# A decayed recurrence in halves of 64 steps, as 64x64 products, in a fused recurrence and expert kernel

## The chip, the cores and the metric

The kernel runs on one core of a Trainium2 chip. The metric is the time of one execution on the device, in microseconds (us). Engines are named as in the profile: PE is TensorE's matrix multiplication, PEld its weight load, DVE is VectorE, ACT is ScalarE, POOL is GpSimd, and SP is SyncE, which here only issues DMAs. [...]

## The reference

Two blocks follow each other. The first is a recurrence with a decaying state for each of 4 batches and 8 heads, with 768 steps and heads of 48; the second sends each of the 3072 resulting rows to one of 16 experts.

```python
B, H, S, D = 4, 8, 768, 48
for t in range(S):
    kt, vt, rt = k[:, :, t], v[:, :, t], r[:, :, t]
    cur = einsum('bhd,bhe->bhde', u[None] * kt, vt)
    y[:, :, t] = einsum('bhd,bhde->bhe', rt, state + cur)
    state = w[None, :, :, None] * state + einsum('bhd,bhe->bhde', kt, vt)

x = y.transpose(0, 2, 1, 3).reshape(B * S, H * D)      # 3072 x 384
# group g of 4 and expert e of 4 by the largest logit; gate = softmax(group) * softmax(expert)
out[token] = gate * (relu(x[token] @ w1[g, e]) @ w2[g, e])   # F = 1024
```

All is fp32.

## The kernel before

**The recurrence.** A tile is 128 steps of one batch with all 8 heads, so there are 6 chunks c times 4 batches b, 24 tiles, in the order of chunks. Two tiles (two batches of one chunk) make a pair g, loaded by three DMAs on SP: r, k and v, two pairs ahead. `SPAN` is 3: powers of the decay are folded into r and k (tables `T1T` and `T2`), so that the state needs a decay only after every third chunk. Heads lie in slots of 64 (`DP`), so that two heads e = 0, 1 fill 128 partitions; `HP` = 4 such double heads hc make up the 8 heads.

One loop over steps s writes the order on every engine by hand (`manual_schedule`): each engine takes its instructions exactly in the order of the program. Step s works on several tiles at different stages:

- `turn(s)` (L569): four transposes of r into bank `pr` and four of scaled k into `pk`. DVE multiplies `pr` by the decay powers into `rT`; ACT copies `pk` to `kT`.
- `own_values` (L560): eight small ACT instructions make `dv`, the part of a step's own k and v. `own_sum` (L556) is the DVE sum it starts from; POOL makes its products `dg` in `own` (L550).
- `rows_T(s-4)` and `row_logits(s-5)`: three transposes of finished rows into `px`, an ACT copy to `xT`, and six short product instructions for the router's logits.
- `back(s-3)` (L637): four transposes of `yT` into `pb`; DVE adds `dv` and writes the rows `xt`.
- `values(s-2)` (L596): the result `py` of a tile. First the state's part, `R` times `rT`, in full 128x128 products (a double head's two 48x48 states on the diagonal of `R`, zeros elsewhere, L605); then the part inside the tile, `vt` times the masked products `am` (L611). ACT copies `py` to `yT` (L616). Then the state's update `pu`, `kh` times `vt` (L622), which DVE adds to `R` (L630 to L635).
- `scores(s-1)` (L582): products of `kT` and `rT` (128 by 128 steps for each head) into two banks `pa`, which DVE multiplies by the mask `later` into `am` (L594).

Every fourth tile a routing follows, spread over the next steps by the dictionary `todo`: `choice` on DVE with one exp on ACT (at s = 9, 13, 17, 21, between `own_values` and `rows_T`), then in the next step `before` (two products into a bank `pre`, ahead of `turn`), `gate` and `place` at the step's end (`place` is the last to read `pre`), and then scatters of rows to DRAM by POOL. Towards the end the routings of the last chunk come two tiles at a time.

**PSUM.** Six banks turn round for everything (`bank`); two more (`route_bank`) hold logits. A new tile takes a bank as soon as all that used it are done:

```python
psum = ctx.enter_context(tc.tile_pool(name="psum", bufs=6, space=bass.MemoryType.PSUM))
rpsum = ctx.enter_context(tc.tile_pool(name="rpsum", bufs=2, space=bass.MemoryType.PSUM))
```

**The experts.** Seventeen items (the first expert in two parts) follow, each as: `columns` (transposes into `px`), `up` (four times, banks `ph`, L506), `down` (three times, bank `po`, L520) and `rows_out` (transposes into `pb`, then a scatter of rows by POOL). The first item is worked on inside the last steps of the recurrence. Weights of the next expert are loaded meanwhile.

Of the kernel before, what the change touches and what calls it, by code (L numbers as in the profile page):

```python
# [8 lines left out]
FP32 = mybir.dt.float32  # L9
# [25 lines left out]
def kernel(  # L35
# [46 lines left out]
    psum = ctx.enter_context(tc.tile_pool(name="psum", bufs=6, space=bass.MemoryType.PSUM))  # L82

    rpsum = ctx.enter_context(tc.tile_pool(name="rpsum", bufs=2, space=bass.MemoryType.PSUM))

    def bank(shape, name):
        return psum.tile(shape, FP32, tag="bank", name=name)
# [72 lines left out]

    first_use = cst([P, 1], "first_use")
# [16 lines left out]
    R = ring([P, HP, P], "R", B)  # L178
# [22 lines left out]
    for t in R:  # L201
        nc.gpsimd.memset(t, 0.0)
# [126 lines left out]
    def route_bank():  # L329

        return rpsum.tile([P, 512], FP32, tag="route", name="rb")
# [144 lines left out]
    def columns(i):  # L476
        xg, w = xgs.pop(i), width(i)
        xe = xes[i] = item_tile(i, [P, KO, room(i)], "xe")
        for ks in (range(0, KO),) if KO * w <= 512 else (range(0, 2), range(2, KO)):
            px = bank([P, len(ks), w], "px")  # L480
            for q, ko in enumerate(ks):
                for j, n in enumerate(parts(i)):
                    nc.tensor.transpose(  # L483
                        px[:, q, P * j : P * j + n], xg[0:n, j, P * ko : P * (ko + 1)], ident[0:n, 0:n]
                    )
            nc.vector.tensor_copy(xe[:, ks[0] : ks[-1] + 1, 0:w], px)  # L486
        ids = item_tile(i, [P, 2], "ids", U32, bufs=4)
        gates = item_tile(i, [P, 2], "gates", bufs=4)
        for j, n in enumerate(parts(i)):
            nc.vector.tensor_scalar(  # L490
                out=ids[0:n, j : j + 1], in0=xg[0:n, j, DM + ROW_ID : DM + ROW_ID + 1], scalar1=float(N),
                scalar2=None, op0=OP.add,
            )
            nc.vector.tensor_copy(gates[0:n, j : j + 1], xg[0:n, j, DM + ROW_GATE : DM + ROW_GATE + 1])
        keys_of[i] = ids, gates

    def up(i, f):
# [5 lines left out]
        ph = bank([P, 2, w], "ph")  # L503
# [8 lines left out]
    def down(i, d):  # L512
# [5 lines left out]
        po = bank([P, w], "po")  # L518
# [6 lines left out]
    def rows_out(i):  # L525
        y, (ids, gates) = yo.pop(i), keys_of.pop(i)
        for j, n in enumerate(parts(i)):
            pb = bank([P, DM], "pb")
# [52 lines left out]

    def scores(n):  # L582
        kT, rT = rkT[n]
        am = ams[n] = pool.tile([P, 2, HP, P], FP32, tag="am", bufs=2, name="am")
        pa = [bank([P, HP, P], f"pa{e}") for e in range(2)]
        for hc in range(HP):
            for e in range(2):
                rows = slice(DP * e, DP * e + D)
                nc.tensor.matmul(  # L589
                    pa[e][:, hc, :], lhsT=kT[rows, hc, :], rhs=rT[rows, hc, :],  # L590
                    start=True, stop=True, skip_group_check=True,
                )
        for e in range(2):
            nc.vector.tensor_mul(am[:, e], pa[e], spread(later, 1, HP))  # L594

    def values(n):  # L596
# [3 lines left out]
        vt, kh = vts[g % (RING + 1)], khs[g % (RING - 1)]  # L600
        rT, am = rkT.pop(n)[1], ams.pop(n)
        py = bank([P, HP, P], "py")
        if c > 0:
            for hc in range(HP):
                nc.tensor.matmul(  # L605
                    py[:, hc, :], lhsT=R[b][:, hc, :], rhs=rT[:, hc, :], start=(hc == 0), stop=False,
                    skip_group_check=True,
                )
        for hc in range(HP):
            for e in range(2):  # L610
                nc.tensor.matmul(  # L611
                    py[DP * e : DP * (e + 1), hc, :], lhsT=vt[:, a, 2 * hc + e, :], rhs=am[:, e, hc, :],
                    start=(c == 0), stop=True, skip_group_check=True,
                )
        yT = yTs[n] = pool.tile([P, HP, P], FP32, tag="yT", bufs=2, name="yT")
        nc.scalar.copy(yT, py)  # L616
        if c == NCH - 1:
            return
        pu = bank([P, HP, D], "pu")
        for hc in range(HP):  # L620
            for e in range(2):
                nc.tensor.matmul(  # L622
                    pu[DP * e : DP * (e + 1), hc, :], lhsT=kh[:, a, 2 * hc + e, :], rhs=vt[:, a, 2 * hc + e, 0:D],
                    start=True, stop=True, skip_group_check=True,
                )
        for e in range(2):
            rows = slice(DP * e, DP * (e + 1))
            state = R[b][rows, :, DP * e : DP * e + D]
            if c == 0:
                nc.vector.tensor_copy(state, pu[rows])  # L630
            elif c % SPAN < SPAN - 1:
                nc.vector.tensor_add(state, pu[rows], state)
            else:
                nc.vector.tensor_add(pu[rows], pu[rows], state)
                nc.vector.tensor_mul(state, pu[rows], spread(w_span[rows, :], 2, D))  # L635
# [55 lines left out]
    for s in range(NT + LAST):  # L691
# [25 lines left out]
        if s < NT:  # L717
            turn(s)
            if s % 2 == 1 and s // 2 + 1 < NP:
# [3 lines left out]
        for n in range(NT):  # L723
            if s == max(n + 1, 2):
                own_values(n)
# [13 lines left out]
        if 0 <= s - 1 < NT:  # L739
            scores(s - 1)  # L740
# [310 lines left out]
```

## Time and profile before

| | us |
|---|---|
| median of 3 runs | 480.31 (479.12 to 485.27) |
| the profiled execution, its own time | 479.58 |
| its span from the first to the last instruction | 477.9 |
| PE busy | 449.7 |
| DVE busy | 159.5 |
| ACT busy | 139.0 |
| POOL busy | 129.5 |

Busy times are sums over an engine's instructions where overlapping ones count once; a matrix product's end is modelled, so PE's busy time also holds short gaps. Line numbers (L605) are those of the kernel before, and names such as `py<-am,vt` say what is written from what. For the pace of TensorE the starts of successive groups in the order of time are more reliable than the lengths of single instructions, which overlap.

### The profile page before, as it was taken

How to read it: one execution, taken by the hardware profiler on the slowest of the kernel's cores; microseconds unless marked ns; L12 is line 12 of the kernel's file. 1: busy time of each engine (PE TensorE's matmuls, PEld its weight loads, DVE VectorE, ACT ScalarE, POOL GpSimd, SP SyncE). 2: the span in 40 equal slices, each digit the busy share in tenths (PEclk: the TensorE clock that was granted, in tenths of full speed). 3: DMA queues.
4: the chain of work that ended last, by engine and by line, in shares of the span. 5: the costliest groups of instructions: out<-in, count | busy, mean ns of one | idle time of the engine just before them, and what ended most of it. 6: DMA issues, size and time to landing. Idle time of an engine off the chain costs nothing. (4 is left out here: it accounts for less than half of the span.)

```text
span 477.9 us, 9090 instructions
## 1 busy us (share of the span) xinstructions
PE 449.7 (94%) x3623; PEld 430.6 (90%) x3623; DVE 159.5 (33%) x478; ACT 139.0 (29%) x418; POOL 129.5 (27%) x135
## 2 busy tenths in 40 slices
PE   3799999999999898999999999999999999999992
PEld 2598888899999798999999999999999999999991
DVE  5546566877778663010110210110110110111000
ACT  2846553564656321111121111111111111111120
POOL 7834536556564042000010210110120110120011
PEclk9969979999999989999999999999999999999997
DMA  9999999983102994565465754755856765666000
GB/s 176 187 190 228 207 227 202 200 155 77 36 35 69 339 335 132 188 239 168 160 190 182 256 184 153 280 201 156 284 190 198 255 188 199 238 202 236 30 22 26
DMA packets 112024, 86.24 MB, mean 180 GB/s; under 512 B 79633, under 2 KB 103568, under 8 KB 111976
## 3 DMA queue, kind: packets, MB, share of 16 engines
q1 hardware_dynamic: 98920, 68.81, 52.1%
q10 hardware_dynamic: 8432, 7.31, 7.1%
q0 software_dynamic: 4624, 9.48, 5.8%
q8 instruction: 30, 0.49, 0.5%
q14 instruction: 18, 0.15, 0.1%
HBM read 69.79 MB, written 16.12 MB: 180 GB/s over the span
## 5 line engine op out<-in xcount | busy, mean ns | idle before, releaser
L534 POOL DMA_INDIRECT out_dram<-yt,ids x32 | 34.1, 1066 | 255.0 <-DVE yt L532 250.4
L506 PE MATMUL ph<-xe,w 128*128 128x128 f32 (+7 forms) x432 | 72.2, 325 | 0.7 <-DVE xe L486 0.7
L520 PE MATMUL po<-hT,w 128*128 128x128 f32 (+7 forms) x432 | 71.4, 322 | 0.0
L506 PEld LDWEIGHTS ph<-xe,w 128*128 128x128 f32 x432 | 69.0, 194 | 1.2 <-DVE xe L486 0.9
L532 DVE TENSOR_SCALAR yt<-pb,gates 128x384 f32<-128x384 f32 (+15 forms) x32 | 18.3, 611 | 153.4 <-PE pb L530 153.4
L520 PE MATMUL po<-hT,rall 128*128 128x240 f32 (+7 forms) x384 | 68.6, 336 | 0.0
L506 PE MATMUL ph<-xe,kall 128*128 128x240 f32 (+7 forms) x384 | 68.4, 335 | 0.0
L520 PEld LDWEIGHTS po<-hT,w 128*128 128x128 f32 x432 | 67.8, 190 | 0.5
L510 ACT ACTIVATE hT<-ph 128x256 f32<-128x256 f32 (+15 forms) x68 | 33.5, 493 | 112.9 <-PE ph L506 112.9
L520 PEld LDWEIGHTS po<-hT,rall 128*128 128x128 f32 x384 | 65.0, 190 | 0.7
L506 PEld LDWEIGHTS ph<-xe,kall 128*128 128x128 f32 x384 | 64.9, 190 | 0.6
L523 ACT COPY yo<-po 128x128 f32<-128x128 f32 (+15 forms) x51 | 16.3, 320 | 127.7 <-PE po L520 127.7
L564 ACT ACTIVATE dv<-vt,du 128x48 f32<-128x48 f32 x192 | 45.8, 324 | 1.1 <-DVE du L558 1.0
L594 DVE TENSOR_TENSOR am<-pa,later 128x512 f32<-128x512 f32 x48 | 30.9, 685 | 9.0 <-PE pa L589 8.7
L486 DVE COPY xe<-px 128x384 f32<-128x384 f32 (+30 forms) x32 | 14.0, 475 | 53.6 <-PE px L483 53.6
L410 POOL DMA_INDIRECT x_sorted<-xt,place_i x24 | 23.8, 990 | 27.9 <-issue 14.0
L589 PE MATMUL pa<-rT,kT 48*128 48x128 f32 x384 | 29.3, 291 | 0.7 <-DVE xt L646 0.7
L611 PE MATMUL py<-am,vt 128*64 128x128 f32 x384 | 29.2, 290 | 0.7 <-DVE am L594 0.6
L553 POOL TENSOR_TENSOR dg<-rall,kall 128x768 f32<-128x768 f32 x12 | 21.9, 1821 | 28.9 <-DVE du L558 28.9
L548 POOL TENSOR_TENSOR kh<-kall,T 128x768 f32<-128x768 f32 (+1 forms) x12 | 21.4, 1788 | 28.0 <-DMA kall<-in_k_dram 9.7
L611 PEld LDWEIGHTS py<-am,vt 128*64 128x64 f32 x384 | 22.7, 143 | 4.7 <-DVE am L594 1.5
L589 PEld LDWEIGHTS pa<-rT,kT 48*128 48x128 f32 x384 | 24.4, 193 | 2.6 <-DVE xt L646 0.9
(128 smaller groups left out, 469.6 us busy)
## 6 DMA issues: line engine op xcount, KB each, us to landing
w<-in_moe_w_dram SPq DMA_DIRECT2D x16, 1536.0 KB, 6.8
kall<-in_moe_w_dram SPq DMA_DIRECT2D x8, 1536.0 KB, 7.1
rall<-in_moe_w_dram SPq DMA_DIRECT2D x8, 1536.0 KB, 6.8
x_sorted<-nothing ACTq DMA_DIRECT2D x4, 1544.0 KB, 10.2
rall<-in_r_dram SPq DMA_DIRECT2D x12, 384.0 KB, 7.2
vt<-in_v_dram SPq DMA_DIRECT2D x12, 384.0 KB, 6.8
kall<-in_k_dram SPq DMA_DIRECT2D x10, 384.0 KB, 6.4
xg<-x_sorted SPq DMA_DIRECT2D x17, 193.0 KB, 6.2
```

What stands on the lines that cost most here:

```text
L410: ins = nc.gpsimd.indirect_dma_start(out=xs_dram, out_offset=bass.IndirectOffsetOnAxis(ap=place_i[:, i : i + 1], axis=0), in_=xt[:, i, :], ...
L506: nc.tensor.matmul(ph[:, q, :], lhsT=w1[:, ko, P * (f + q) : P * (f + q + 1)], rhs=xe[:, ko, 0:w], start=(ko == 0), stop=(ko == KO - 1), s ...
L510: nc.scalar.activation(hTs[i][:, f : f + 2, 0:w], ph, AF.Relu)
L520: nc.tensor.matmul(po, lhsT=w2[:, fo, P * d : P * (d + 1)], rhs=hT[:, fo, 0:w], start=(fo == 0), stop=(fo == FO - 1))
L532: nc.vector.tensor_scalar(out=yt[0:n], in0=pb[0:n], scalar1=gates[0:n, j : j + 1], scalar2=None, op0=OP.mult)
L534: ins = nc.gpsimd.indirect_dma_start(out=out, out_offset=bass.IndirectOffsetOnAxis(ap=ids[0:n, j : j + 1], axis=0), in_=yt[0:n], in_offset ...
L548: engine.tensor_mul(khs[g % (RING - 1)][:, a0:a1, :, 0:D], kts[g % RING][:, a0:a1], spread(T2[m], 1, a1 - a0))
L553: nc.gpsimd.tensor_mul(dg, rts[g % RING][:, :, :, 0:D], kts[g % RING])
L564: nc.scalar.mul(dv[:, h, :], vts[g % (RING + 1)][:, a, h, 0:D], dvs[g][:, a, h : h + 1])
L589: nc.tensor.matmul(pa[e][:, hc, :], lhsT=kT[rows, hc, :], rhs=rT[rows, hc, :], start=True, stop=True, skip_group_check=True,)
L594: nc.vector.tensor_mul(am[:, e], pa[e], spread(later, 1, HP))
L611: nc.tensor.matmul(py[DP * e : DP * (e + 1), hc, :], lhsT=vt[:, a, 2 * hc + e, :], rhs=am[:, e, hc, :], start=(c == 0), stop=True, skip_gr ...
```

## The change

A tile of 128 steps keeps its loads, its transposes and its tables. Inside it the recurrence goes in two halves q of 64 steps:

- Scores and values are formed only inside a half: 64x64 products (48 rows for the scores), and each product names one quarter of the array by the half of the partitions that it reads and the half that it writes. `am` has half the width, and the mask is a 64-wide one for both halves, `later_half`, filled by two ACT copies.
- The state is needed at the tile's start and in its middle. `R` becomes a ring of three states for each batch, without the empty diagonal blocks; `from_state` multiplies it by `rT` in 64x64 products, in the two diagonal quarters.
- The state's update leaves `values` and becomes `update(s)`, right after `turn(s)` in a tile's first step, with two products (one for each half) and two DVE additions (one in the last chunk, where the kernel before had none). It shares two banks with the scores of the same step.
- `from_state(s-1)` is called ahead of `scores(s-1)`, one step before `values` completes the same banks `py`, of which there are now two for a tile, one for each half. Each half is copied by ACT on its own.
- `own_values(n)` runs at s = n+2 and no longer at s = max(n+1, 2).
- PSUM is one pool of four names with two slots each: "bank" (pr, pk, px, pb, pre and others in the recurrence), "scores", "values" and "route". The expert stage is spread over the same names.

The diff, with the main parts:

```diff
-    psum = ctx.enter_context(tc.tile_pool(name="psum", bufs=6, space=bass.MemoryType.PSUM))
-    rpsum = ctx.enter_context(tc.tile_pool(name="rpsum", bufs=2, space=bass.MemoryType.PSUM))
-    def bank(shape, name):
-        return psum.tile(shape, FP32, tag="bank", name=name)
+    psum = ctx.enter_context(tc.tile_pool(name="psum", bufs=2, space=bass.MemoryType.PSUM))
+    def bank(shape, name, tag="bank"):
+        return psum.tile(shape, FP32, tag=tag, name=name)
...
+    HALF = P // 2
+    later_half = cst([P, HALF], "later_half")
+    for a in range(2):
+        rows = slice(HALF * a, HALF * (a + 1))
+        nc.scalar.copy(later_half[rows, :], later[rows, rows])
...
-    R = ring([P, HP, P], "R", B)
+    R = [ring([P, HP, DP], f"R_{b}", 3) for b in range(B)]
-    for t in R:
-        nc.gpsimd.memset(t, 0.0)
+    for t in sum(R, []):
+        nc.gpsimd.memset(t[:, :, D:DP], 0.0)
...
-            px = bank([P, len(ks), w], "px")
+            px = bank([P, len(ks), w], "px", "route" if i > 0 else "bank")
-        ph = bank([P, 2, w], "ph")
+        ph = bank([P, 2, w], "ph", "bank" if f % 4 == 0 else "scores")
-        po = bank([P, w], "po")
+        po = bank([P, w], "po", "values")
...
+    def update(n):
+        c, b = tiles[n]
+        g, a = n // 2, n % 2
+        vt, kh = vts[g % (RING + 1)], khs[g % (RING - 1)]
+        pu = [t[:, HP * HALF :].rearrange("p (c d) -> p c d", c=HP) for t in both]
+        halves = 2 if c < NCH - 1 else 1
+        for hc in range(HP):
+            for q in range(halves):
+                half = slice(HALF * q, HALF * (q + 1))
+                for e in range(2):
+                    nc.tensor.matmul(
+                        pu[q][DP * e : DP * (e + 1), hc, :], lhsT=kh[half, a, 2 * hc + e, :],
+                        rhs=vt[half, a, 2 * hc + e, 0:D], start=True, stop=True, skip_group_check=True,
+                    )
+        for q in range(halves):
+            old, new = state(n, q)[:, :, 0:D], state(n, q + 1)[:, :, 0:D]
+            if c == 0 and q == 0:
+                nc.vector.tensor_copy(new, pu[q])
+            elif q == 0 or c % SPAN < SPAN - 1:
+                nc.vector.tensor_add(new, pu[q], old)
+            else:
+                nc.vector.tensor_add(pu[q], pu[q], old)
+                nc.vector.tensor_mul(new, pu[q], spread(w_span, 2, D))
...
+    def from_state(n):
+        c, b = tiles[n]
+        rT = rkT[n][1]
+        py = pys[n] = [bank([P, HP, HALF], f"py{q}", "values") for q in range(2)]
+        for q in range(2):
+            if c == 0 and q == 0:
+                continue
+            half = slice(HALF * q, HALF * (q + 1))
+            for hc in range(HP):
+                for e in range(2):
+                    rows = slice(DP * e, DP * (e + 1))
+                    nc.tensor.matmul(
+                        py[q][rows, hc, :], lhsT=state(n, q)[rows, hc, :], rhs=rT[rows, hc, half],
+                        start=(hc == 0), stop=False, skip_group_check=True,
+                    )
...
     def scores(n):
-        am = ams[n] = pool.tile([P, 2, HP, P], FP32, tag="am", bufs=2, name="am")
-        pa = [bank([P, HP, P], f"pa{e}") for e in range(2)]
+        am = ams[n] = pool.tile([P, 2, HP, HALF], FP32, tag="am", bufs=2, name="am")
+        pa = [t[:, 0 : HP * HALF].rearrange("p (c t) -> p c t", c=HP) for t in both]
...
+                for q in range(2):
+                    half = slice(HALF * q, HALF * (q + 1))
+                    nc.tensor.matmul(
+                        pa[e][half, hc, :], lhsT=kT[rows, hc, half], rhs=rT[rows, hc, half],
+                        start=True, stop=True, skip_group_check=True,
+                    )
...
     def values(n):
+                    nc.tensor.matmul(
+                        py[q][DP * e : DP * (e + 1), hc, :], lhsT=vt[half, a, 2 * hc + e, :], rhs=am[half, e, hc, :],
+                        start=(c == 0 and q == 0), stop=True, skip_group_check=True,
+                    )
-        nc.scalar.copy(yT, py)
+        for q in range(2):
+            nc.scalar.copy(yT[:, :, HALF * q : HALF * (q + 1)], py[q])
...
         if s < NT:
             turn(s)
+        if s <= NT:
+            both = [bank([P, HP * (HALF + D)], f"pa{e}", "scores") for e in range(2)]
+        if s < NT:
+            update(s)
...
-            if s == max(n + 1, 2):
+            if s == n + 2:
                 own_values(n)
...
         if 0 <= s - 1 < NT:
+            from_state(s - 1)
             scores(s - 1)
```

## The prediction

> **What bounds the kernel now.** I read the page first (which engine, which stretch), then the sums over windows, then the order in time of one step of the recurrence, and last one step in which ScalarE and VectorE are late.
>
> ```profile
> span 477.9 us, 9090 instructions
> PE 449.7 (94%) x3623; PEld 430.6 (90%) x3623; DVE 159.5 (33%) x478; ACT 139.0 (29%) x418; POOL 129.5 (27%) x135
> ...
> PEclk9969979999999989999999999999999999999997
> ...
> L594 DVE TENSOR_TENSOR am<-pa,later 128x512 f32<-128x512 f32 x48 | 30.9, 685 | 9.0 <-PE pa L589 8.7
> ...
> L611 PE MATMUL py<-am,vt 128*64 128x128 f32 x384 | 29.2, 290 | 0.7 <-DVE am L594 0.6
> ```
> TensorE bounds the kernel in both stages: the experts from about 180 us on, which the change touches only in the names of PSUM slots, and before that 24 tiles of recurrence, one a step. Each fp32 product is two instructions (384 for 192), so I count instructions.
>
> ```profile
> 22.33:32.57 10.24, 9.63 (x72) 8.64 (x73) 5.40 (x10) 5.77 (x22) 4.60 (x5) 0.50 1.16 186
> ...
> 66.70:73.53 6.83, 6.83 (x34) 6.52 (x35) 1.88 (x4) 2.75 (x10) 0.29 (x1) 0.50 1.20 199
> 114.27:120.66 6.39, 6.33 (x83) 5.96 (x81) 6.00 (x20) 3.26 (x12) 5.04 (x4) 1.00 0.02 9
> ```
> These are sums by window: length, busy PE, PEld, DVE, ACT, POOL, then the granted clock. Twice the clock was halved, after TensorE had been idle (18.8 to 21.7; 0.73 us and more just before 65.06). The third line is an undisturbed step: PE full, DVE nearly so.
>
> A plain step in order of time (start, length, engine):
>
> ```profile
> 120.77 0.61 PE L575 MATMUL pr<-ident,rall 128*128 128x128 f32 x4
> ...
> 121.22 0.60 PE L575 MATMUL pk<-ident,kh 128*128 128x128 f32 x4
> ...
> 121.65 0.49 PE L438 MATMUL px<-ident,xt 128*128 128x128 f32 x3
> ...
> 121.98 0.74 PE L443 MATMUL rb<-gw,xT 128*128 128x20 f32 x6
> ...
> 122.57 0.64 PE L645 MATMUL pb<-ident,yT 128*128 128x128 f32 x4
> ...
> 123.04 1.06 PE L605 MATMUL py<-rT,R 128*128 128x128 f32 x8
> ...
> 124.03 1.09 PE L611 MATMUL py<-am,vt 128*64 128x128 f32 x16
> ...
> 124.95 0.62 PE L622 MATMUL pu<-vt,kh 128*64 128x48 f32 x16
> 125.22 0.59 ACT L616 COPY yT<-py 128x512 f32<-128x512 f32 x1 [0.56 <-PE py L611]
> 125.50 0.97 PEld L589 LDWEIGHTS pa<-rT,kT 48*128 48x128 f32 x16
> 125.50 1.16 PE L589 MATMUL pa<-rT,kT 48*128 48x128 f32 x16
> ...
> 126.60 0.44 PE L575 MATMUL pr<-ident,rall 128*128 128x128 f32 x2
> ```
> From start to start: turn 0.88 (0.93 after a step with pa), px 0.33, logits 0.59, pb 0.47, state product 0.99, py 0.92, pu 0.55, pa 1.10; 5.83 together, 5.87 in most steps. Nothing waits: yT is copied while TensorE already does pu and pa, because py may lie in one of six banks.
>
> A step with a routing choice, on DVE and ACT:
>
> ```profile
> 116.84 0.23 DVE L363 TENSOR_REDUCE mx<-rb 128x20 f32<-128x80 f32 x1
> ...
> 119.52 0.23 DVE L376 TENSOR_TENSOR ex<-rb,mx 128x80 f32<-128x80 f32 x1
> ...
> 119.79 0.27 ACT L377 ACTIVATE ex<-ex 128x80 f32<-128x80 f32 x1 [1.94 <-DVE ex L376]
> 119.97 0.46 ACT L439 COPY xT<-px 128x384 f32<-128x384 f32 x1
> 120.33 0.59 ACT L616 COPY yT<-py 128x512 f32<-128x512 f32 x1
> ```
> The choice holds DVE for 2.9 us, ACT waits in order for its exp, and yT comes 6.06 us after the step's start (114.27), when TensorE has finished the whole step. Here that costs almost nothing.
>
> [...] two-at-once groups take 57 ns an instruction (L611) against 124 for L605, single starts lie in pairs 6 ns apart, and mode changes cost 0.05 to 0.15 us. Four at once is not shown. [...] The halved stretches here are 10.24 and 6.83 us[...].
>
> **The change part by part.** *Products.* Instructions a tile: before 8+16+16+16, after 32 each for state, values, update, scores. In L622 a pair of 64-column loads repeats every 58 ns in the trace[...]. Four at once I take at the same 58 to 60 ns a round: 8 rounds are 0.48, 0.6 with a mode change, for update and values; 0.6 for scores with the change back. Bounds: 0.5, and 0.95 if only two ever run together. from_state uses only the two diagonal quarters: 16 rounds of 58, 0.95. Sum 2.75 against 3.56: TensorE saves 0.8 us a step, 0.3 in the first and last four tiles (the first now have half a state product, the last half an update). About 15 us in all if no wait came.
>
> *Wait A, the banks of py.* from_state(s-1) needs both "values" banks, which values(s-2), just ahead of it on TensorE, has filled. So TensorE waits for the result (0.29 after the last start, from L622's 0.27), the first half's copy (0.36, from 0.46 at 384 columns and 0.36 at 240), 0.06 for the signal and 0.05 for weights: about 0.65 a step more. Behind it stand from_state, scores and the next step. This takes most of the 0.8.
>
> *Wait B, update against the masks.* update(s) comes right after turn and needs the "scores" banks that the am products of the step before are reading. At half width these are 0.42 each (0.685 at 512, 0.553 at 384 columns); they end 1.0 after the step's start, turn 0.93. Cost 0.13. rT follows at 1.6, when update ends, so px, which takes pr's bank, does not wait. A plain step: 0.93+0.13+0.6+0.33+0.59+0.47+0.6+0.65+0.95+0.6 = 5.85. No gain.
>
> *Choice steps (s = 9, 13, 17, 21).* DVE has the adds of update first (to 2.5), then 2.9 us of choice: 5.4. exp, xT, then yT's first half end near 6.3; only then from_state (0.95) and scores (0.6): 7.95, 2.1 more than plain.
>
> *Steps with pre first (10, 14, 18, 22).* pre keeps one of the two "bank" slots until the place product at the step's end, so pr, pk, px, pb share one. pr ends at 0.94; pk waits for rT (1.99); update to 3.0; px waits for kT (3.36); pb waits for xT, which stands behind eight dv on ACT (5.5); values to 6.6, wait A, from_state to 8.2, scores 8.8. That is 2.5 over 6.3. The next step loses 0.3 because gate and place hold DVE ahead of am.
>
> Four steps thus take 5.87+7.95+8.8+6.15 = 28.8, four times 115.2 for s = 8 to 23. Before they took 103.6 (from step starts at 52.6 and 156.2), 4.6 of it through the halved clock: 11.6 more.
>
> *Clock.* Each choice step leaves TensorE idle for 2.7 us, like the gaps of 2.9 and 3.0 that were followed by halving, and the pre step after it idles again. Step 10 and 11 lost 4.6 us to 6.8 us of half clock; with waits as cover I take 3 us for each of four: 12. Bounds 0 and 20.
>
> *The rest.* Early on, update(3) waits for am(1), which stands behind the reduce of dg on DVE (until 22.2): one part step later, 1.5. own_values one step later frees yT(0) on ACT, but that only lets TensorE reach the same wait. v is needed two steps earlier; its loads land 4.3 to 13.2 us after issue and are issued four steps ahead, so no wait. The two later_half copies (0.2 each) fall into ACT's 4.4 idle us before L254, the twelve memsets of R into POOL's 2.05 idle us before L548; without that cover 0.5 each. DVE saves 0.5 a step on am, not its bound. The tail loses the pu and wide state work but keeps its waits for rows: -0.5. Expert stage: ph alternates over two pairs of banks, po has two, px and pb meet two that were emptied microseconds before: 0.
>
> Sum against the profiled execution (479.6, span 477.9): 479.6+11.6+12+1.5-0.5 = 504.2. The median of the runs shown is 0.7 above it: 505.
>
> **Rivals.** *No halved clock* (0.20): [...] for it speaks a gap of 0.77 at 94.9 that did nothing, against it all gaps near 3. 505-12 = 493. *Only two at once* (0.17): both instructions of a product go to the same quarter, and if the queue doesn't pass them, three groups stay at 0.95: 1.05 a step over 23 steps, 24: 529. For it: no trace shows four. Against: in L589 the second row group starts 6 ns after the first. The change would then not do what it says. *The products win* (0.10): if a bank is handed on without that order, so that the added wait a step averages under 0.5 us, the 0.8 us remain. With none, 20 steps by 0.8: 464; it decides from about 0.8 downwards. Against it: TensorE takes its queue in order and both banks are full.
>
> **How the numbers follow.** Forecast 0.53 (497 to 516). The range 487 to 529 leaves out the winning case and some of the two-at-once case. Faster by over 2% (about what a measurement can tell from no change): 0.08; within: 0.10 (part of the last and of the no-halving case); slower: 0.82.
>
> **What would show it.** Right: update, values, scores spaced 15 ns an instruction, from_state 29; ACT yT ahead of the state product as TensorE's largest wait; choice and pre steps of 8 to 9 us; more halved clock between 60 and 155 us; expert stage as long as before. Wrong: products at 30 ns, or plain steps near 5 us with no wait on yT.

## The result and the profile after

530.75 us median (521.03 to 537.07) against 479.72 (477.15 to 485.27), so the kernel got slower by 51 us in the medians. The ratio is 1.095, 95% interval 1.076 to 1.114; ratios here and below leave out slow runs, which of this kernel are 533.60 and 537.07 (granted clock 0.893 and 0.898; the fast ones, 521.03 and 527.90, had 0.940 and 0.915). Forecast were 505 in a range of 487 to 529 and 0.82 for slower. The profile below is of the execution of 537.07 us, the longest: its sums lie some 6 us above the median and 9 and 16 us above the two shortest executions, and by the granted clocks it holds more half clock than these.

The page of the kernel after, and two groups from its list by shape:

```profile
span 535.3 us, 12495 instructions
PE 473.4 (88%) x5319; PEld 444.9 (83%) x5319; DVE 147.8 (28%) x478; ACT 141.6 (26%) x444; POOL 128.6 (24%) x143
...
PEclk9979875985977866779999999999999999999997
...
L652 DVE TENSOR_TENSOR am<-pa,later_half 128x256 f32<-128x256 f32 x48 | 18.2, 419 | 56.8 <-PE pa L647 53.3
...
L632 PE MATMUL py<-rT,R 64*64 64x64 f32 x704 | 32.8, 256 | 25.2 <-ACT yT L670 21.0
L664 PE MATMUL py<-am,vt 64*64 64x64 f32 x768 | 20.9, 254 | 4.0 <-issue 4.0
```

TensorE's share fell from 94% to 88%, and there is a wait in the L632 row that no row of TensorE had before: from_state waits 21 us for yT. The digits of PEclk are below 9 in 13 of the first 20 slices (before in 3). The stretches at half clock as windows (length, busy PE, PEld, DVE, ACT, POOL, granted clock, DMA share, GB/s):

```profile
30.63:37.46 6.83, 6.59 (x111) 5.72 (x112) 2.81 (x7) 2.76 (x10) 1.81 (x1) 0.50 1.16 178
...
115.97:133.00 17.03, 15.64 (x241) 13.62 (x238) 6.37 (x18) 4.75 (x18) 5.52 (x4) 0.50 0.19 39
...
221.80:235.40 13.60, 13.60 (x66) 13.60 (x65) 6.72 (x38) 2.49 (x9) 5.83 (x6) 0.50 0.24 88
sum 102.38, PE 91.22 PEld 82.09 DVE 37.38 ACT 27.44 POOL 30.99; mean PE 9.12 PEld 8.21 DVE 3.74 ACT 2.74 POOL 3.10
```

102 us ran at half clock, against 20.5 before (10.24, 6.83, and one of 3.41 at 169.1). A plain step in order of time:

```profile
137.09 0.66 PE L579 MATMUL pr<-ident,rall 128*128 128x128 f32 x4
...
138.11 0.68 PE L602 MATMUL pa<-vt,kh 64*64 64x48 f32 x32
...
138.73 0.55 PE L442 MATMUL px<-ident,xt 128*128 128x128 f32 x3
...
140.26 0.69 PE L664 MATMUL py<-am,vt 64*64 64x64 f32 x32
...
141.05 0.65 ACT L670 COPY yT<-py 128x256 f32<-128x256 f32 x2
141.47 1.00 PEld L632 LDWEIGHTS py<-rT,R 64*64 64x64 f32 x31 [0.65 <-ACT yT L670]
...
142.45 0.64 PE L647 MATMUL pa<-rT,kT 48*64 48x64 f32 x30
143.01 0.20 PEld L579 LDWEIGHTS pr<-ident,rall 128*128 128x128 f32 x2
```

From start to start: update 0.61, from_state 0.87 for 29 of its 32 instructions, scores 0.57. From values to from_state 1.21 pass, half of it the bracketed wait for yT. The step is 5.93 (137.09 to 143.02). A choice step, where it ends late:

```profile
114.00 0.23 DVE L380 TENSOR_TENSOR ex<-rb,mx 128x80 f32<-128x80 f32 x1
114.27 0.27 ACT L381 ACTIVATE ex<-ex 128x80 f32<-128x80 f32 x1 [1.85 <-DVE ex L380]
114.44 0.46 ACT L443 COPY xT<-px 128x384 f32<-128x384 f32 x1
...
114.80 0.65 ACT L670 COPY yT<-py 128x256 f32<-128x256 f32 x2
...
115.23 1.27 PE L632 MATMUL py<-rT,R 64*64 64x64 f32 x29 [2.52 <-ACT yT L670]
```

The step began at 108.84; from_state comes 6.39 after that, behind exp, xT and yT on ScalarE, as worked out.

The span of this execution grew by 57.4 us. By starts of pr, steps 0 to 3 take 23.3 us (before 19.1), 4 to 7 31.6 (24.3), 8 to 22 133.8 (98.2), and from step 23 to the first expert's po it is 40.2 (29.0). The expert stage behind is as long as before.

### The profile page after: what moved, and what is told of

The parts are those of the page before. It is cut to its first block, busy times and chain, and to the rows that moved or that the text cites. A ratio compares the mean times of both kernels' runs of the same rounds, so it can differ in the third digit from the quotient of the medians.

```text
span 535.3 us, 12495 instructions
## 1 busy us (share of the span) xinstructions
PE 473.4 (88%) x5319; PEld 444.9 (83%) x5319; DVE 147.8 (28%) x478; ACT 141.6 (26%) x444; POOL 128.6 (24%) x143
## 5 line engine op out<-in xcount | busy, mean ns | idle before, releaser
L510 PE MATMUL ph<-xe,w 128*128 128x128 f32 (+7 forms) x432 | 74.8, 333 | 0.7 <-DVE xe L490 0.7
L510 PEld LDWEIGHTS ph<-xe,w 128*128 128x128 f32 x432 | 71.6, 202 | 1.2 <-DVE xe L490 0.9
L632 PE MATMUL py<-rT,R 64*64 64x64 f32 x704 | 32.8, 256 | 25.2 <-ACT yT L670 21.0
L632 PEld LDWEIGHTS py<-rT,R 64*64 64x64 f32 x704 | 28.9, 166 | 28.7 <-ACT yT L670 24.3
L583 ACT COPY kT<-pk 128x512 f32<-128x512 f32 x24 | 14.0, 584 | 83.4 <-PE pk L579 75.6
L652 DVE TENSOR_TENSOR am<-pa,later_half 128x256 f32<-128x256 f32 x48 | 18.2, 419 | 56.8 <-PE pa L647 53.3
L664 PEld LDWEIGHTS py<-am,vt 64*64 64x64 f32 x768 | 16.9, 160 | 9.4 <-issue 9.1
L664 PE MATMUL py<-am,vt 64*64 64x64 f32 x768 | 20.9, 254 | 4.0 <-issue 4.0
```

The costliest lines, as they stand in the source:

```text
L510: nc.tensor.matmul(ph[:, q, :], lhsT=w1[:, ko, P * (f + q) : P * (f + q + 1)], rhs=xe[:, ko, 0:w], start=(ko == 0), stop=(ko == KO - 1), s ...
L632: nc.tensor.matmul(py[q][rows, hc, :], lhsT=state(n, q)[rows, hc, :], rhs=rT[rows, hc, half], start=(hc == 0), stop=False, skip_group_chec ...
L652: nc.vector.tensor_mul(am[:, e], pa[e], spread(later_half, 1, HP))
L664: nc.tensor.matmul(py[q][DP * e : DP * (e + 1), hc, :], lhsT=vt[half, a, 2 * hc + e, :], rhs=am[half, e, hc, :], start=(c == 0 and q == 0) ...
```

## The experiments

The runs fell to four chips, called A to D here. The kernel before takes 478.7 to 482.4 us on each of them; that a kernel with halves can differ between chips came out only in the last run, and on which chip the changed kernel itself ran isn't on record. Its interval, 1.076 to 1.114, is wide: of its variants only experiments 5, 8 and 12 lie wholly below it, 11 touches it. What 1 to 4, 7, 9 and 10 changed is therefore read from their steps, and differences of medians are rough.

**1. Scores ahead of from_state (chip A)**, to cover the wait for yT:

```
-            from_state(s - 1)
-            scores(s - 1)
+            for part in (scores, from_state) if s < NT - 1 else (from_state, scores):
+                part(s - 1)
```

> Edit of the changed kernel: scores(s-1) ahead of from_state(s-1), except for the last two tiles. Theory W (the wait for the copies of yT is what eats the products' saving): the copies now lie beside scores (0.57 us), so the wait ahead of from_state falls from 0.6 to about 0.1 us in a plain step, and by 0.5 us in the choice steps; 22 steps by 0.5 is 11 us, with fewer halved windows up to 18: 512 to 520 us against the 530.75 of the changed kernel. Rival C (the halved clock is the cost and comes from the choice and pre steps alone): plain steps shrink but the halved stretches stay, 519 to 522. Rival F (TensorE waits for its own instructions, 'issue'): these waits, 3.8, 2.1 and 4.3 us long, stay where they are.

Measured: 520.24 us (514.86 to 523.46), ratio 1.088 (1.081 to 1.095). The plain step falls from 5.93 to 5.46, and what is left of the wait, from the list of waits over 15 to 240 us:

```profile
PEld py L632 <- ACT yT L670: 6.8, 12, 2.6
```

The same line of the changed kernel:

```profile
PEld py L632 <- ACT yT L670: 24.3, 22, 3.1
```

24.3 us in 22 waits become 6.8 in 12 (the third number is the longest); half clock 58 us, in its shortest execution (514.86). Wait A is real and of the size worked out; a gain in the whole time isn't shown (1.081 to 1.095 lies inside the changed kernel's interval).

**2. pre's products at the end of their step (chip A):**

```
-                ...extend([("first", before), ("last", gate), ("last", place)])
+                ...extend([("last", before), ("last", gate), ("last", place)])
```

> Edit of the changed kernel: the two products of pre move from ahead of turn to the end of the step, so that pre no longer keeps one of the two bank slots while pr, pk, px and pb need them. Theory W with the slot part of the prediction: each of the four steps loses its waits of pk (1.2) and pb (about 1.3): 4 by 2.5 is 10 us, a few more if the clock recovers sooner: 515 to 521. If the slots don't matter (the step is long because the clock is halved in it): 528 to 531.

Measured: 516.05 us (515.42 to 517.19), ratio 1.078 (1.072 to 1.084). The four pre steps, from pr to pr, take 7.4, 7.6, 6.1 and 7.8 us in place of 11.0, 11.4, 10.9 and 11.4; half clock 58 us.

**3. The choice behind the values on all engines (chip A):**

```
-        run("choice")
         if 0 <= s - 4 < NT:
...
             values(s - 2)
+        run("choice")
```

> Edit of the changed kernel: the routing choice comes after values on every engine, so that the copies of yT no longer stand behind the choice's exp on ScalarE. Theory W: the wait ahead of from_state in the four choice steps falls from 2.6 to 0.6 us: 8 us, and as the long gaps end, some of the halved clock behind them goes: 510 to 523. Against it: VectorE then holds the next am behind the choice, so the wait moves to update in the next step and little is won: 527 to 531.

Measured: 532.92 us (520.71 to 536.05), with no interval for it: the time decides nothing. The last three choice steps are 9.1, 9.0 and 8.2 in place of 9.5, 9.5 and 9.0. ScalarE no longer stood behind exp, and yet yT came late:

```profile
112.83 1.01 POOL L414 DMA_INDIRECT x_sorted<-xt,place_i  x1 [0.16 <-issue]
...
113.20 0.69 PE L664 MATMUL py<-am,vt 64*64 64x64 f32 x32
...
114.15 0.97 POOL L414 DMA_INDIRECT x_sorted<-xt,place_i  x1 [0.30 <-issue]
...
115.81 0.65 ACT L670 COPY yT<-py 128x256 f32<-128x256 f32 x2 [1.84 <-remote]
```

The last of the values started at 113.67. In other steps the event of their completion follows after 0.1 to 0.3; here it came 2.06 later, and so (2.03 to 2.06) in three of the four choice steps, each with two scatters of GpSimd beside it. The first choice step, without scatters, has no such delay. Neither theory had this. The changed kernel has the same delay in the same three steps (2.06 to 2.09); there it is covered by the exp, behind which yT starts 2.17 to 2.31 after the last of the values.

**4. Products without use before from_state (chip A)**, ten in choice steps and two in the others, so that TensorE is not idle while it waits:

```
+            for _ in range(10 if s in (9, 13, 17, 21) else 2):
+                nc.tensor.matmul(both[0][:, 448:512], lhsT=ident, rhs=ident[:, 0:64], ...)
```

> Edit of the changed kernel: idle TensorE time ahead of from_state is filled with products nobody reads (ident times 64 columns of ident, into unused columns of a scores bank): 10 in the four choice steps, 2 in all others. It removes no wait. Theory C (the halved clock costs what the waits themselves don't): the halved stretches behind the choice steps get fewer and the time falls by 8 to 20 us, to 511 to 523. Rival (the clock isn't what counts[...]): 530 to 535, the fillers' mode changes making it a little slower.

Measured: 525.35 us (522.71 to 527.25), ratio 1.095 (1.088 to 1.102): in the time no difference from the changed kernel is shown. The profiled execution (527.25) has 58 us of half clock, that of the changed kernel (537.07) 102; the granted clock is 0.938 to 0.947 in all four executions, in the changed kernel's 0.893 to 0.940. From 129 to 187 us it is full. That shows steps at full clock: one choice step with its pre step, in order of time:

```profile
147.44 0.65 ACT L670 COPY yT<-py 128x256 f32<-128x256 f32 x2
...
149.41 0.43 PE L385 MATMUL pre<-ohe,later 128*128 128x64 f32 x2
149.90 0.61 PE L579 MATMUL pr<-ident,rall 128*128 128x128 f32 x4
151.39 0.63 PE L579 MATMUL pk<-ident,kh 128*128 128x128 f32 x4 [0.88 <-DVE rT L581]
...
158.26 0.66 PE L579 MATMUL pr<-ident,rall 128*128 128x128 f32 x4
```

The choice step began at 141.47 and ends with pre at 149.41, 7.94; the pre step lasts until 158.26, 8.85. In the profile of the changed kernel the same two take 8.60 and 11.82, of which 1.5 and 8.4 are at half clock. The differences, 0.7 and 3.0, are less than half of these stretches, so the clock can account for all of them.

**5. The first two edits together (chip B):**

> The two edits that gained alone, together: scores ahead of from_state (10.5 us alone), and the products of pre at the end of their step (14.7 us alone). If they remove different idle time of TensorE, the gains add: 506 us, plain steps of 5.45 and pre steps of 6 to 7 us. Rival: both fill the same gap (the wait for yT or the half clock that follows it), so the second adds little: 512 to 516 us, pre steps over 7.5. A rival that the product of halves can still win needs under 480, and nothing so far points to it.

Measured: 494.29 us (491.11 to 503.01), ratio 1.029 (1.026 to 1.031), the best of all, yet slower than before. By medians that is 11 us better than the two gains added (10.5 and 14.7); on another chip the surplus is gone (experiment 12).

**6. The kernel before with the division of PSUM alone (chip B)**: four names of two slots, products and order as before.

```
-    psum = ...tile_pool(name="psum", bufs=6, ...)
+    psum = ...tile_pool(name="psum", bufs=2, ...)
...
-        pa = [bank([P, HP, P], f"pa{e}") for e in range(2)]
-        py = bank([P, HP, P], "py")
-        pu = bank([P, HP, D], "pu")
+        pa = [bank([P, HP, P], f"pa{e}", "scores") for e in range(2)]
+        py = bank([P, HP, P], "py", "values")
+        pu = bank([P, HP, D], "pu", "values")
```

> The kernel before with one part of the change alone: the eight PSUM banks divided into four names of two slots each (pr, pk, pb, px and the rest in one, pa in one, py and pu in one, the logits in one), all products and their order as before. Theory: TensorE's queue mostly finds its bank free, since the prediction put the wait for a bank at 0.13 us a step: 480 to 485 us, plain steps of 5.9. Rival: two slots for pr, pk, pb and px hold TensorE for a copy in each step (0.3 to 0.5 us a step), and the gaps bring the half clock: 488 to 500 us, so that a fifth or more of the loss would lie in the division and not in the halves.

Measured: 524.58 us (522.89 to 528.11), ratio 1.091 (1.087 to 1.094). Theory wrong, rival right and too small: 44 us from names of slots. From the list of waits:

```profile
PE px L437 <- ACT kT L578: 11.7, 16, 0.7
```

In the order of the kernel before px comes right behind pk and, with two slots, takes pr's or pk's. Each such wait is at most 0.7 us; with the gaps came 58 us of half clock. So the 44 us can't be taken over as a share of the changed kernel's loss: there the update stands between pk and px, and this wait occurs once, for 2.5 us.

**7. The zeros later (chip B):**

```
-        if s in (3, 5, 7, 9):
-            zero_places(s // 2 - 1)
+        if s == 9:
+            for j in range(4):
+                zero_places(j)
```

The reason for it, in the changed kernel's order of time:

```profile
26.05 0.68 PE L632 MATMUL py<-rT,R 64*64 64x64 f32 x15 [0.82 <-ACT yT L670]
...
30.87 0.36 PE L632 MATMUL py<-rT,R 64*64 64x64 f32 x1 [4.15 <-issue]
```

TensorE stops in the midst of a group, with nothing to wait for that the profile shows. There are three such gaps, from start to start 4.37, 3.78 and 2.33 us; the third lies in step 8. Counting all of TensorE's instructions (loads, products and the few that wait), they come ahead of number 706, 1474 and 1986, a multiple of 256 apart, and a packet of 16 KB in queue q8, of the kind "instruction", starts 2.5 to 2.9 us before each of them ends (28.41, 50.51 and 64.58 us).

> The changed kernel with the four writes of zeros into x_sorted (1.5 MB each) all issued in step 9 and not in steps 3, 5, 7 and 9, so that the DMA engines are less loaded in the first 75 us. Theory: TensorE ran dry of instructions there because the packets that fetch them waited behind other packets: the gaps that end by nothing but issue (4.4, 3.8 and 2.3 us in the changed kernel) shrink below 1 us each, with the half clock behind them: steps 0 to 7 last 7 to 12 us less in all. The scatters behind the zeros start later, which may give back up to all of it in the end; the verdict is in steps 0 to 7. Rival: the number of instructions alone does it [...]: the gaps stay at 2 us and more.

Measured: 521.49 us (517.81 to 524.96), ratio 1.084 (1.077 to 1.091). The same stretch, 20 to 64.84 us, first in the changed kernel, then here:

```profile
20.00:64.84 44.84, 33.08 (x775) 28.95 (x775) 17.48 (x39) 20.61 (x75) 20.00 (x13) 0.85 1.10 201
```

```profile
20.00:64.84 44.84, 36.99 (x1011) 32.61 (x1002) 25.09 (x62) 25.65 (x92) 27.00 (x17) 0.96 0.97 164
```

1011 product instructions in place of 775 in the same time, and no gap of this kind among steps 0 to 7, which last 44.2 us and not 54.8. It isn't the chip: experiment 8, on B too and with the zeros in their old places, has the three gaps ahead of the same numbers and takes 54.5 us. Step 9, where ScalarE issues all four writes, then takes 19.5 us, and a gap of 2.56 us comes at 95.38, ahead of number 3010 (four times 256 behind 1986), so part of the gain is lost again. At the same count of instructions the gaps went with the load on DMA (share 0.97 over this stretch, in the changed kernel 1.10).

**8. The choice behind the values, and scatters two a step (chip B):**

```
-                    at = s + 3 + (i // 2 if n == FOUR * B - 1 else i)
+                    at = s + 3 + i // 2
```

> The choice behind the values, as in the third experiment, and the four scatters of a group in the two steps behind its places, two a step, so that none falls into the next group's choice step. Theory: the completion of the values that came 2.1 us after their last start in the steps 13, 17 and 21 (0.2 to 0.4 in all others) is due to the scatters on GpSimd at that time; it falls to 0.2 to 0.4, the choice step from 9.1 to 7 us, and the time to 520 to 526 us. Rival: it is due to the choice itself or to the logits' bank; then the 2.1 us stay and the time is that of the third experiment, 533 us.

Measured: 511.62 us (508.94 to 518.62), ratio 1.061 (1.058 to 1.064). Completions come after 0.2 to 0.3 and the last three choice steps take 6.7. It looked like the theory; but the seventh experiment, on the same chip and with its scatters untouched, also has 0.23 in steps 13, 17 and 21, at an offset to the scatters like that of experiment 3. So it proves nothing on scatters' places.

**9. The edits 1, 2, 3 and 8 together (chip C):**

> The four edits together: scores ahead of from_state, pre's products at their step's end, choice behind the values, scatters two a step behind the places. Theory: the changed kernel lost by waits that its order and its two-slot names make, and each edit takes one of them away: 511.6 (choice and scatters) less 10.5 (scores) less 14.7 (pre) gives 486 us; the two edits of the fifth experiment gained 11 us more than their sum, since with each gap a stretch of half clock goes as well, so 475 to 490 us, no step from 9 on above 9 us. Rival: the stalls for instructions and the half clock behind the group starts stay, and the edits share one gap: 490 to 495 us, no better than the fifth experiment.

Measured: 512.89 us (510.53 to 517.01), ratio 1.069 (1.060 to 1.078). A miss: 19 us worse than experiment 5 on chip B, 6 worse than the same kernel on D (experiment 12). The choice steps are down to 5.5 to 6.0, but steps 11, 15 and 19, where four scatters now stand in a row, take 10.2 to 10.4. There the completion is 2.7 to 3.0 late.

**10. pre in the logits' bank (chip C)**, its products first in their step as in the changed kernel:

```
-            pre = held["pre"] = bank([P, T, GE], "pre")
+            pre = held["pre"] = rb[:, 448 : 448 + T * GE].rearrange("p (i e) -> p i e", i=T)
```

> The changed kernel with one edit: pre has no bank of its own but 64 columns of the logits' bank that its step holds anyway; its products stay first in their step. Theory: in the pre steps pre held one of the only two slots that pr, pk, px and pb share, from the step's start until its end, so that each of those four waited for the copy of the one before; without it the pre steps fall from 11 to 7 to 8.5 us, and the time to 514 to 520 us, as with the products at the end of the step. Rival: it is the place, TensorE waiting at the step's start for ohe from VectorE behind the choice: the pre steps stay above 10 us and the time at 527 to 533.

Measured: 531.0 us (525.99 to 531.18), ratio 1.108 (1.099 to 1.117). In its profile (525.99 us) the pre steps take 6.5, 5.9, 7.2 and, at half clock almost throughout, 10.0. Step 14 begins with:

```profile
113.01 0.60 PE L579 MATMUL pr<-ident,rall 128*128 128x128 f32 x4
113.45 0.60 PE L579 MATMUL pk<-ident,kh 128*128 128x128 f32 x4
```

pk follows pr after 0.44, in the changed kernel's step 14 after 1.94 (118.31 and 120.25, at half clock), in experiment 4 after 1.49. So pre's slot did hold the step, as the prediction had it. The time did not follow, and the 514 to 520 us of the theory are a miss: the scatters now stand beside the values in steps 11, 15 and 19 too, with completions 1.94 to 1.96 late, and the other runs of this kernel are 5 us longer than the profiled one. What those 5 us are stays open.

**11. Whole products in the changed kernel's order (chip C)**: the halves alone undone, with products over 128 steps, a block-diagonal state in two slots, one update a tile, at the places and with the PSUM names of the changed kernel, but that `pu` has a slot of "values" and a tile's py one and not both.

```
-            for q in range(2):
-                half = slice(HALF * q, HALF * (q + 1))
...
+        py = pys[n] = bank([P, HP, P], "py", "values")
+                    py[:, hc, :], lhsT=state(n)[:, hc, :], rhs=rT[:, hc, :], start=(hc == 0), ...
+        pu = bank([P, HP, D], "pu", "values")
```

> The changed kernel with the halves alone undone: products over 128 steps as before (scores 128x128, state block-diagonal, one update a tile), but at the places, in the PSUM names and with the state of several slots of the changed kernel. Theory: the products of halves save what the prediction said (2.75 against 3.56 us a step, 0.8 x 24 = 19 us), and the stalls for instructions, 10.5 us plus the half clock behind them, are gone since there are fewer instructions: 530.75 + 19 - 10 to 15 = 535 to 540 us, so the loss against the kernel before lies in order and PSUM. Rival: the halves themselves are the loss (two waits for their copies, instructions, half clock): under 510 us.

Measured: 510.83 us (508.57 to 512.41), ratio 1.067 (1.058 to 1.076). Neither number: in the medians 20 us better than the changed kernel, 32 worse than before. A plain step:

```profile
120.06 0.67 PE L594 MATMUL pu<-vt,kh 128*64 128x48 f32 x16
...
122.40 1.09 PE L647 MATMUL py<-am,vt 128*64 128x128 f32 x16
123.43 1.16 PE L619 MATMUL py<-rT,R 128*128 128x128 f32 x8
124.51 1.16 PE L632 MATMUL pa<-rT,kT 48*128 48x128 f32 x16
125.61 0.66 PE L573 MATMUL pr<-ident,rall 128*128 128x128 f32 x4
```

Update 0.80, values 1.02, from_state 1.09, scores 1.10: 4.0 us, for which halves need 2.7. The plain step is 6.57 and the changed one's 5.93 is better by 0.64, its wait included. But TensorE has hardly a gap here: there is no wait for yT, half clock is 34 us in all, and after 26 us TensorE never stops in the midst of a group as in experiment 7. So the halves win their plain step and lose more than that elsewhere; the clock and the fetch of instructions are where the two profiles differ, but how much each costs isn't separated. Between the two ratios (1.076 to 1.114, and 1.058 to 1.076) the intervals just touch, by the ratios the difference is 14 us and not 20, and the runs may have been on different chips, so its size is rough.

**12. Experiment 5 once more, unchanged (chip D):**

> The kernel of the fifth experiment once more, unchanged, on whatever chip it falls to. In all kernels run so far, the completion of a tile's values beside two scatters on GpSimd came 1.9 to 3.0 us after their last start on two of the chips, and 0.2 to 0.3 on a third, where the fifth, seventh and eighth experiment ran, at the same offset between scatter and products. Theory: it belongs to the chip and not to the edits; on another chip than that of the fifth experiment the completions are late (1.9 us and more) in the steps with two scatters, and the time is 500 to 512 us; on the same chip it is 494 again. Rival: it belongs to the kernel (places in memory, offsets of the scatters): 0.2 to 0.3 and 494 us on every chip.

Measured: 506.44 us (503.96 to 507.19), ratio 1.047 (1.039 to 1.055), for the same kernel that took 494.29 on chip B. The same step in the profiled executions (501.23 and 507.00 us), first on chip B:

```profile
102.67 0.69 PE L664 MATMUL py<-am,vt 64*64 64x64 f32 x32
102.69 1.01 POOL L414 DMA_INDIRECT x_sorted<-xt,place_i  x1 [0.15 <-issue]
...
103.19 0.65 PE L647 MATMUL pa<-rT,kT 48*64 48x64 f32 x32
```

and on chip D:

```profile
103.88 0.69 PE L664 MATMUL py<-am,vt 64*64 64x64 f32 x32
103.96 1.01 POOL L414 DMA_INDIRECT x_sorted<-xt,place_i  x1
...
104.39 0.51 PE L647 MATMUL pa<-rT,kT 48*64 48x64 f32 x14
...
105.31 0.35 PE L647 MATMUL pa<-rT,kT 48*64 48x64 f32 x4 [0.41 <-issue]
106.07 0.31 PE L647 MATMUL pa<-rT,kT 48*64 48x64 f32 x3 [0.41 <-issue]
...
106.83 0.46 PE L647 MATMUL pa<-rT,kT 48*64 48x64 f32 x11 [0.44 <-issue]
```

The scores' 32 instructions go in one burst on chip B and trickle out over 2.5 us on chip D. The completions in six steps with two scatters come 1.9 to 2.5 late on D, 0.2 to 0.3 on B. The other profiles agree: with two scatters at such places beside the values, those of experiments 1 to 4, 9 and 10 on A and C have the delay, those of 5, 7 and 8 on B don't. The delay goes with the chip, not with the edits: this theory held. It follows that experiments 5, 7 and 8 are flattered against the rest (by 12 us for the fifth), and that the fifth's surplus over the sum of its parts, 505.5 by medians, is gone on D.

## Why the prediction was right, and which sizes were off

**Products: right.** Update, values and scores at 0.57 to 0.61, four at once, from_state at 0.92: 2.7 us where 2.75 was worked out. The rival of only two at once fell with the first group.

**Waits: right in the plain step, in part by luck in the choice steps.** Wait A was priced at 0.65 and is 0.65 in the plain step shown (0.51 for the product, 0.65 for its weights); experiment 1 moved it and took 0.47 from the step. The plain step is 5.93 for 5.85. Choice and pre steps, worked out as 7.95 and 8.8, are 7.94 and 8.85 where the clock is full (experiment 4, whose added products stand inside the wait). In three choice steps the late completion ends almost with the chain through exp (2.06 to 2.09 against 2.17 to 2.31 after the last of the values), and experiment 3 shows that it would have held the step by itself: the prediction had one of two causes of the same length. That pre keeps a slot for its whole step was shown by experiments 2 and 10. The step behind it was taken as 6.15 and is 6.9 to 7.6: in the changed kernel's profile two of these steps begin at half clock, and in experiment 4, where step 19 takes 7.72 at full clock, from_state waits with a completion 1.9 late beside that step's scatters. The profile before doesn't show this delay: its completions come after 0.3 to 0.4, in step 23 with a scatter beside the values too.

**The clock: right in kind, too small.** Twelve us were taken, with bounds of 0 and 20. Steps 8 to 22 grew by 35.6 in the profiled execution, and the step sum explains 11.6 for one step more: 24 are left, of which 2.3 are the third stall for instructions. The other 22 stand beside 64 us of half clock in these steps, where before there were 6.8; that they are the clock's is a subtraction and not a measurement, and in the shorter executions, at a higher granted clock, the part is smaller. The mis-sized sentence is "I take 3 us for each of four": it took one halving for each group of four steps, of the size seen before. (Of the 4.6 us that it read there some 1.3 belong to step 11, which began at 75.84, after the clock was back at 73.53; step 10 alone lost 3.2.) But a halved step is a longer step with the same waits (pk's for rT is 0.88 at half clock, at 120.25, and at full clock in experiment 4), and one stretch from 115.97 lasted 17 us. Nor was TensorE wholly idle ahead of each halving: in experiment 2 it was busy for 1.61 and 1.27 us of the 3.41 us (the shortest halved stretch of these profiles) ahead of those at 113.84 and 127.49, each with a gap of 2.1 to 2.5 us. What sets off a halving is not shown. The range's top, 529, came from another case; the median is 1.75 above it, the two executions of the ratio lie below.

**Early: missed.** 1.5 us were taken for steps 0 to 7; it is 11.5. The failed step is the count of instructions: it went into the products' time, and that they must be fetched was put at nothing. TensorE had 3623 product instructions before and has 5319 now, with as many loads, and queue q8 moved 30 packets before and 43 now; two of the three stalls, 8.1 us, lie in these steps, and experiment 7 removed them by moving DMA load.

**Tail: wrong sign.** -0.5 was taken, +11.2 measured. "Keeps its waits for rows" left out the clock: 24.4 us of the tail's time run at half clock (197.3 to 197.9, 201.3 to 211.5, 221.8 to 235.4), against 3.4 before. Experiment 1, with the same work in its tail and 6.8 us of half clock, takes 30.9 there, experiment 8 29.6, so most of the 11.2 is not fixed to the halves.

**The sum by cause.** Experiment 11 divides the loss: about 32 us for order, PSUM names and the update ahead with whole products, about 14 to 20 more for the halves, in spite of 1.3 us of product time saved in each full step. No experiment takes the 32 apart, but the steps show where they lie: the four pre steps take 42.4 us together, before 26.6, and the tail 35.0, before 29.0, both with half clock in them; plain steps take 6.57, before 5.87. So the largest piece is in the steps in which pre keeps a slot, with the halvings that fall into them. No version tried beats the kernel before.

## What to carry to other kernels

Making an engine's products shorter did not help where the step was held by the emptying of PSUM by other engines (a plain step's 3.56 us of products became 2.7, but 0.65 went into a wait for a copy, and the step is 5.93 for 5.87); count how many tiles a name's slots let be in flight before and after, and who is queued between filling and refilling. A gap of 2 to 3 us cost itself and then, where a halved stretch followed it in these runs, a third to a half of that stretch (3.0 us for 8.4, 0.7 for 1.5), so price a chain of gaps and not one. And with 32 small instructions in place of 16 large ones more had to be fetched (43 packets of 16 KB in place of 30) while the DMA engines were busy (share 1.10 from 20 to 64.84 us), and TensorE stood still for 4.37, 3.78 and 2.33 us.

## What the runs showed of the hardware

- In the changed kernel's plain step (137.09 to 143.02) the instructions of update and values, whose products name all four quarters of the array, start four at a time, 7 ns apart, every 58 ns, with 48 columns (L602) as with 64 (L664); those of from_state, which name two quarters, two at a time every 58 ns. An fp32 product is two such instructions (L664: 768 for 384 products).
- Where products of one form follow those of another, the first two starts come later than the pace of their groups, by 0.13 to 0.20 us together: before, L611 starts 205 ns after the last of L605 and its second pair 154 ns after the first, where 112 and 109 are the pace (124.03), and in the changed kernel values start 202 ns after the last of pb and their second four after 107, where 109 and 58 are (140.26). The prediction has 0.05 to 0.15 for this.
- From the end of a copy that TensorE waits for to its first load 0.05 us pass (before, yT to pb at 21.70; changed, yT to from_state at 141.47), and the first two starts behind it lie 0.05 to 0.06 further apart than the rest; the prediction took 0.06 and 0.05.
- Products that are ready do not pass one that waits: only with scores placed ahead of from_state do they fill its wait, 24.3 us in all before and 6.8 then (experiment 1).
- TensorE stopped inside a group three times in the changed kernel, for 4.37, 3.78 and 2.33 us from start to start, ahead of instructions a multiple of 256 apart and with a 16 KB packet of the instruction queue 2.5 to 2.9 us before the end; the DMA engines' share in these gaps was 1.11, 1.26 and 1.13. With the zeros written later (experiment 7) steps 0 to 7 have none. That TensorE ran dry of instructions is read from this.
- Beside two scatters in a row on GpSimd, TensorE's instructions and its completions are held back by 1.9 to 3.0 us on three chips (A, C and D), and not on chip B, where the same kernel is 12 us faster (494.29 and 506.44). Whole products aren't free of it: in experiment 11, on C, completions beside one scatter come after 1.0 in place of 0.3. The kernel before takes 478.7 to 482.4 on all four; in its profile only one scatter, in step 23, starts beside values, and the others start after them. What differs between the chips is open, and so is what TensorE waits for.
